# Block-sparse attention feeding a gated FFN on one core: attention scheduled in half batches, with smaller gathers issued earlier and a copied second key tile

## The chip, the cores and the metric

One core of one Trainium2 chip. Times are device microseconds (us) of that core, of whole executions; a profile is of one such execution. The engines are called here as in the profile: PE (TensorE matmuls), PEld (its weight loads), DVE (VectorE), ACT (ScalarE), POOL (GpSimd) and SP (SyncE, which here only issues DMAs).

## The reference, cut to what matters

Four batches, eight heads, 768 positions, head size 64. A query block of 32 positions sees its neighbours, the first and the last block, and three sampled blocks; the first and the last query block see everything. The attention output, 3072 tokens of 512, goes through a gated FFN.
```python
def _attn_ref(q, k, v, sampled_blocks):          # (4, 8, 768, 64) each
    scores = np.matmul(q, k.transpose(0, 1, 3, 2)) / np.sqrt(D)
    mask = np.abs(blk_i - blk_j) <= 1            # blocks of 32
    mask = mask | (blk_i == 0) | (blk_j == 0) | (blk_i == n_blocks - 1) | (blk_j == n_blocks - 1)
    for qb in range(n_blocks):
        for kb in sampled_blocks[qb]:            # three per query block
            mask[qb * block:(qb + 1) * block, kb * block:(kb + 1) * block] = True
    # ... softmax over the masked scores
    return np.matmul(attn, v)

def _moe_ref(x, w_gate, w_val, w_out):           # x (3072, 512), w (512, 1536), (1536, 512)
    gate = 1.0 / (1.0 + np.exp(-(x @ w_gate)))
    return gate * (x @ w_val) @ w_out
```

## The kernel before

Four head pairs of four batches are 16 units of attention. For each unit PE transposes K and Q (`turn`), POOL gathers the sampled key blocks and the "second key tile" of each query tile (the two blocks that follow its first key tile, the first and the last block) into `kg`, and likewise for the values into `vg`. Five score steps (`x` = 0 to 4) each go through an exponential on ACT, the first three also through a mask multiply on DVE. `values` multiplies with V for three of the six query tiles, `x_turn` transposes the result for the FFN. The order in which the program emits the instructions of one engine matters: in the traces below they run in it.

```python
    def gather_k(u):
        t = work.tile([128, NKI, BLK], f16, tag="kg", bufs=2, name="kg")
        data = kT[u].bitcast(u32).rearrange("p (n r) -> p n r", r=BLK // 2)
        for i in range(2):
            nc.gpsimd.indirect_copy(
                # ... 45 of the 90 blocks: 720 words a partition, from data by idx[:, i, 0:3]
            )

    def gather_v(u):
        # ... two indirect_copy, one a head: 30 blocks, 960 words a partition

    def scores(u, x):
        # ...
        if x < 3:
            for i in range(2):
                # ...
                mm(i, 0, kT[u][:, t * 128 : t * 128 + 128], qs, n)
                c = (3 * NQ + 4 * t) * BLK
                mm(i, n, kg[u][:, c : c + 128], qs, n)      # the second key tile, gathered

    def pieces(b):                                          # attention of one whole batch
        # ...
        def prep(u):
            return [
                lambda: (turn(u, "k"), gather_k(u)),
                lambda: (turn(u, "q"), gather_v(u)),
            ]
        r += prep(first)
        for u in us:
            # ... score steps of u, values of u - 1, prep(u + 1) if u is not the last

    spread_v(0, 0)
    spread_v(0, 1)
    head = pieces(0)
    for i, s in enumerate(head):                            # all of batch 0 first
        s()
        if i in (3, 6, 9):
            load_w(i // 3 - 1)
    # ... loads of batch 1 and of the output weights

    for b in range(B):                                      # FFN of batch b beside attention of b + 1
        g = 2 * b
        if b == 0:
            items = [s for two in zip(ins(0), ins(1)) for s in two] + outs(0)
        else:
            items = mix(ins(g), lag) + mix(ins(g + 1), outs(g))
        lag = outs(g + 1)
        # ...
        steps = pieces(b + 1) if b + 1 < B else []
        lo, hi = (0.5, 0.97) if b == 0 else (0.05, 0.95)
        # ... the steps are strewn among the items between the shares lo and hi
```

The softmax here doesn't subtract the row's maximum and nothing guards it: scores larger than these inputs give would overflow.

## Time and profile before

| | before |
|---|---|
| median of the three runs before the prediction, and the two fast ones | 419.06 us; 415.95 and 419.06 (the third took 766.75 us) |
| profiled execution | 416.7 us, mean granted clock 0.913 |
| first FFN matmul | 85.6 us |
| PE waiting for the gathered keys | 57.1 us |

The last line is the total of the view of waits. The first view is from part 2 of the page: PE's busy tenths in 40 slices of 10.4 us, and the granted clock of PE.

```profile
PE   1140656899744876969189999959699999999984
...
PEclk9999756589968999998869999979699999999999
```

PE is nearly full only from the 22nd slice on, with dips at the 27th and the 29th. The clock line dips where PE had been idle. It says nothing of the first slices: the clock record in the trace begins at 44.2 us, and the view counts what stands before as full speed. The windows view cuts the same execution at the first FFN matmul and at the end of the last attention; its columns are the stretch, its length, busy time of each engine with its count of instructions, the granted clock, the DMA share and GB/s.

```profile
0.00:85.60 85.60, 38.76 (x633) 29.53 (x634) 34.56 (x84) 23.94 (x25) 44.48 (x48) 0.82 0.80 114
85.60:351.40 265.80, 216.71 (x2647) 134.04 (x2646) 121.50 (x230) 101.06 (x143) 101.95 (x86) 0.92 0.48 82
351.40:416.70 65.30, 58.01 (x309) 29.93 (x307) 20.78 (x35) 12.28 (x25) 0.00 (x0) 1.00 0.12 41
```

The middle has PE busy 216.7 of 265.8 us at a clock of 0.92. Who PE waited for from the first FFN matmul on (total us, times, longest):

```profile
PE st L296 <- POOL kg L262: 34.8, 8, 9.9
```

One such wait, in order of time (start, us, what it was, and in brackets the idle time before it and what ended it):

```profile
295.54 0.39 PE L296 MATMUL st<-qz,kg 128*128 128x256 f16 x1 [4.67 <-POOL kg L262]
...
296.15 1.48 PE L434 MATMUL gv<-x,wg 128*128 128x384 f16 x4
297.43 1.48 PE L434 MATMUL gv<-x,wv 128*128 128x384 f16 x4
```

After 4.67 us of idle PE is slow: four matmuls of 384 columns take 1.28 us from start to start (296.15 to 297.43) where an undisturbed group takes 0.65. The spacing is back to normal after 300 us, so this wait cost some 7 us: 4.67 us idle and about 2.3 us of slow work (an estimate: half of the 4.7 us until then). A key gather is short (1.20 us for 720 words), but 2.1 to 2.4 us stand before each in which POOL does nothing else, mostly put down to "issue". POOL needs 14.3 us a unit in the stretch where it is busiest:

```profile
129.05 1.21 POOL L262 INDIRECT_COPY kg<-kT,idx 128x720 uint32 x1 [2.35 <-issue]
...
143.36 1.21 POOL L262 INDIRECT_COPY kg<-kT,idx 128x720 uint32 x1 [2.07 <-DVE xs L410]
...
157.98 1.44 POOL L262 INDIRECT_COPY kg<-kT,idx 128x720 uint32 x1 [2.08 <-DVE xs L410]
```

These are the first key gathers of the last three units of batch 1; the three other gathers of each unit stand between them. They follow each other with no room for PE to run ahead, and the attention of a batch is only about 22 us of PE work: this stretch runs at POOL's pace.

### The profile page before, as it was taken

What the parts mean: (1) busy time and instruction counts of PE and PEld (TensorE: products, weight loads), DVE (VectorE), ACT (ScalarE), POOL (GpSimd) and SP (SyncE); (2) the same over time, 40 slices, a digit from 0 to 9 for tenths busy, and PEclk for the clock granted to TensorE, in tenths of its full rate; (3) what the DMA queues carried; (4) which work ended last, traced back from release to release, by engine and by line L of the source; (5) the groups of instructions that cost most, each with busy time, mean ns of one, the idle gap of its engine ahead of it and who ended that gap; (6) DMA issues with size and microseconds to landing.
All of it is one profiled execution on the core that took longest, in us unless ns stands there. A gap on an engine that the chain in (4) does not pass through costs nothing.

```text
span 416.7 us, 8409 instructions
## 1 busy us (share of the span) xinstructions
PE 313.5 (75%) x3584; PEld 193.5 (46%) x3584; DVE 176.8 (42%) x349; ACT 137.3 (33%) x193; POOL 146.4 (35%) x133
## 2 busy tenths in 40 slices
PE   1140656899744876969189999959699999999984
PEld 1030534655422654635056666525366665555541
DVE  6230534433422564444135655435266554333321
ACT  1040343423324444225125454125154551222200
POOL 8415533680043544850443359024433410000000
PEclk9999756589968999998869999979699999999999
DMA  9979750299940000898500109666101000101102
GB/s 123 208 156 172 114 95 2 36 158 212 199 91 2 2 2 2 118 208 178 140 0 28 27 27 146 144 154 140 37 27 27 27 4 26 50 25 28 50 28 76
DMA packets 67046, 34.23 MB, mean 82 GB/s; under 512 B 28352, under 2 KB 63936, under 8 KB 67008
## 3 DMA queue, kind: packets, MB, share of 16 engines
q0 software_dynamic: 36368, 14.16, 28.8%
q1 hardware_dynamic: 30640, 19.53, 19.4%
q8 instruction: 28, 0.46, 0.5%
q14 instruction: 10, 0.08, 0.1%
HBM read 28.57 MB, written 6.29 MB: 84 GB/s over the span
## 4 chain that ended last, share of the span: by engine, by line
PE 53%; issue 12%; POOL 11%; DMA 9%; DVE 8%; ACT 3%; SPq 2%; DVEq 0%; POOLq 0%
PE gv L434 23%; PE py L454 14%; PE st L296 7%; DMA v<-va 7%; POOL kg L262 6%; PE pv L357 6%; POOL vg L277 3%; SPq L144 2%; ACT pt L331 2%; PE ptr L245 2%; DVE pt L342 2%; DVE kT L251 1%; DMA va<-in_v_dram 1%; POOL va L135 1%; DVE y L463 1%
## 5 line engine op out<-in xcount | busy, mean ns | idle before, releaser
L331 ACT ACTIVATE pt<-st 128x1024 f16<-128x1024 f32 (+1 forms) x80 | 79.8, 1002 | 148.3 <-PE st L296 148.2
L296 PE MATMUL st<-qz,kg 128*128 128x64 f16 (+1 forms) x448 | 45.5, 228 | 62.9 <-POOL kg L262 57.1
L342 DVE TENSOR_TENSOR pt<-pt,mask 128x1024 f16<-128x1024 f16 (+1 forms) x64 | 39.4, 636 | 115.5 <-ACT pt L331 115.4
L277 POOL INDIRECT_COPY vg<-v,idx 128x960 uint32 x32 | 57.8, 1807 | 76.6 <-issue 48.1
L445 DVE SCALAR_TENSOR_TENSOR h<-tg,gv 128x384 f16<-128x384 f32 x96 | 53.1, 553 | 74.0 <-PE gv L434 66.3
L434 PE MATMUL gv<-x,wg 128*128 128x384 f16 x384 | 82.4, 339 | 0.0
L434 PE MATMUL gv<-x,wv 128*128 128x384 f16 x384 | 80.7, 334 | 1.8 <-DVE h L445 1.0
L443 ACT ACTIVATE tg<-gv 128x384 f32<-128x384 f32 x96 | 47.0, 490 | 100.1 <-PE gv L434 86.7
L262 POOL INDIRECT_COPY kg<-kT,idx 128x720 uint32 x32 | 39.4, 1232 | 109.8 <-issue 51.4
L454 PE MATMUL py<-wo,h 128*128 128x512 f16 x288 | 75.5, 389 | 2.9 <-DVE y L463 2.9
L296 PEld LDWEIGHTS <-kg 128*128 128x128 f16 x448 | 26.5, 106 | 79.8 <-POOL kg L262 64.3
L434 PEld LDWEIGHTS <-wv 128*128 128x128 f16 x384 | 38.4, 100 | 32.7 <-issue 10.4
L434 PEld LDWEIGHTS <-wg 128*128 128x128 f16 x384 | 36.8, 101 | 25.3 <-issue 3.8
L296 PE MATMUL st<-qz,kT 128*128 128x256 f16 (+1 forms) x192 | 39.0, 277 | 11.9 <-DVE qz L256 9.6
L454 PEld LDWEIGHTS <-h 128*128 128x128 f16 x288 | 26.3, 100 | 27.7 <-issue 5.7
L357 PEld LDWEIGHTS <-pt 128*32 128x32 f16 (+2 forms) x1280 | 32.3, 107 | 8.9 <-DVE xs L410 3.5
L357 PE MATMUL pv<-vg,pt 128*32 128x65 f16 (+2 forms) x896 | 31.7, 207 | 0.0
L357 PE MATMUL pv<-va,pt 128*64 128x65 f16 (+1 forms) x384 | 25.7, 207 | 2.7 <-DVE xs L410 2.7
L296 PEld LDWEIGHTS <-kT 128*128 128x128 f16 x192 | 17.9, 110 | 12.9 <-DVE kT L251 5.5
L135 POOL DMA_DIRECT2D va<-in_v_dram x24 | 21.2, 911 | 0.0
L463 DVE TENSOR_SCALAR y<-py 128x512 f32<-128x512 f32 x24 | 16.5, 688 | 11.0 <-PE py L454 10.9
L410 DVE TENSOR_TENSOR xs<-pv,rz 128x384 f16<-128x384 f32 x32 | 17.8, 557 | 1.1
(44 smaller groups left out, 154.1 us busy)
## 6 DMA issues: line engine op xcount, KB each, us to landing
v<-va SPq DMA_DIRECT2D x128, 99.0 KB, 2.4
out_dram<-y SPq DMA_DIRECT2D x20, 256.0 KB, 2.0
k<-in_k_dram POOLq DMA_DIRECT2D x16, 192.0 KB, 6.2
q<-in_q_dram POOLq DMA_DIRECT2D x16, 192.0 KB, 6.8
va<-in_v_dram POOLq DMA_DIRECT2D x24, 128.0 KB, 5.4
wg<-in_moe_w_gate_dram POOLq DMA_DIRECT2D x3, 512.0 KB, 5.7
wv<-in_moe_w_val_dram POOLq DMA_DIRECT2D x3, 512.0 KB, 7.5
wo<-in_moe_w_out_dram POOLq DMA_DIRECT2D x3, 512.0 KB, 12.2
```

Source lines behind the costliest of these rows:

```text
L135: nc.gpsimd.dma_start(va[b % 2][:, m, :, 0:D], v[b, :, m * 128 : m * 128 + 128].rearrange("h p d -> p h d"),)
L262: nc.gpsimd.indirect_copy(t.rearrange("p n r -> p (n r)") .bitcast(u32) .rearrange("p (n r) -> p n r", r=BLK // 2)[:, 45 * i : 45 * i + 45 ...
L277: nc.gpsimd.indirect_copy(vg[u % 2][hd] .rearrange("p n e -> p (n e)") .bitcast(u32) .rearrange("p (n e) -> p n e", e=VE // 2)[:, :, 0 : D ...
L296: nc.tensor.matmul(st[:, bank, col : col + n], keys, qs, start=True, stop=True)
L331: nc.scalar.activation(pt[:, 0:w], st.rearrange("p a n -> p (a n)")[:, 0:w], AF.Exp, scale=SCALE)
L342: nc.vector.tensor_tensor(pp, pp, mk.unsqueeze(2).to_broadcast([128, 2 * nt, 2, nq]), op=ALU.mult)
L357: nc.tensor.matmul(pvv[rows, tl, hd, :], pr, val[:, 0:65], start=first[0], stop=False, skip_group_check=True, **({} if pos is None else {" ...
L434: nc.tensor.matmul(t, w[:, i, f * 128 : (f + 1) * 128], xT[g, i], start=(i == 0), stop=(i == NP - 1),)
L443: nc.scalar.activation(tg, pgs.pop((g, f)), AF.Tanh, scale=0.5)
L445: nc.vector.scalar_tensor_tensor(h_, tg, 1.0, pvv_.pop((g, f)), op0=ALU.add, op1=ALU.mult)
L454: nc.tensor.matmul(pys[g, tt], hts[g, f][:, tt * 128 : (tt + 1) * 128], wo[:, f], start=(f == 0), stop=(f == NF - 1),)
L463: nc.vector.tensor_scalar_mul(y, pys.pop((g, tt)), 0.5)
```

## The change

Its intent: put only half of batch 0's attention before the FFN, run attention half a batch ahead of the FFN from then on, and take gathers off PE's path. A unit is now a half batch and a head pair (32 units of three query tiles). The second key tile is copied by DVE (`kb`) and the second value tile by DMA (`second_v`), so the gathers hold sampled blocks only, one gather for keys and one for values of both heads; they are emitted two units ahead, and K is transposed three units ahead.

```diff
-    def spread_v(b, half):
+    def spread_v(b, hh, eng):
         for a in range(4):
-            for s in range(4):
+            for s in range(3):
...
+    def second_v(b, half):
+        n = 3 if half == 0 else 2
+        t = work.tile([128, 3, H, VE], f16, tag="vb", bufs=2, name="vb")
...
+    load_qk(0, 0, "k")
+    load_qk(0, 0, "q")
+    for i in range(NZ):
+        nc.vector.memset(qz[i], 0.0)
+        if i < 2:
+            nc.vector.memset(va[i][:, :, :, D:VE], 1.0)
+            nc.gpsimd.memset(v4[i], 0.0)
...
-            t = work.tile([128, S], f16, tag="kT", bufs=3, name="kT")
+            t = work.tile([128, S], f16, tag="kT", bufs=5, name="kT")
...
+            s = work.tile([128, NT - 1, 128], f16, tag="kb", bufs=5, name="kb")
+            tb = t.rearrange("p (n r) -> p n r", r=BLK)
+            nc.vector.tensor_copy(
+                s[:, :, 0:64], t.rearrange("p (m c) -> p m c", c=128)[:, 1:NM, 0:64]
+            )
...
-        t = work.tile([128, NKI, BLK], f16, tag="kg", bufs=2, name="kg")
+        n = 3 * (RS[half][1] - RS[half][0]) + 2
+        t = work.tile([128, 38 * BLK], f16, tag="kg", bufs=4, name="kg")
...
-                mm(i, n, kg[u][:, c : c + 128], qs, n)
+                mm(col + n, kb[b, p][:, min(i, NT - 2)], qs, n)
...
+    def ahead(w):
+        r = []
+        b, i = divmod(w, 2 * NP)
+        for b2, p in ((b + 1, i - 5), (b, i + 3)):
+            if 0 <= p < NP and 0 < b2 < B:
+                r.append(lambda b2=b2, p=p: turn(b2, p, "k"))
...
+        if w + 2 < NW and w + 2 >= NP:
+            r.append(lambda: (gather_k(w + 2), gather_v(w + 2)))
...
+    spread_v(0, 1, nc.scalar)
+    second_v(0, 0)
+    load_w(1)
...
+    for g in range(2 * B):
+        items = mix(ins(g), outs(g - 1) if g else [])
...
+        todo = steps(g + 1) if g + 1 < 2 * B else []
+        lo, hi = 0.04, 0.92
```

## The prediction

> **What bounds the kernel now.** TensorE, but only part of the time. In the windows view 220 to 267.6 us has TensorE busy 45.8 of 47.6 us at clock 1.00. The head is not so: 0 to 80 us has it busy 35 us, with the clock at 0.59 to 0.69 after 40 us, and the first FFN matmul starts at 85.6 us, because all of batch 0's attention comes first, paced by gathers and loads. 112 to 220 us is broken too. PE waits for the kg gather: 27.6 us before 120 us, 20.5 us from 120 to 220, then 4.3 and 4.7 us in the batch at 267 to 353. The Trainium skill (TensorE: Matmul & The Clock Gate, Part 1) says an idle window of about 3.4 us halves the clock. The trace agrees: after the 4.7 us wait that ends at 295.5 us, 8 FFN matmuls take 2.56 us instead of 1.30.
>
> **Dense work.** From undisturbed spacings: FFN input 1.30 us per 8 matmuls, x96 = 125; output 0.87 us per 4, x72 = 62; attention about 11 us per half batch. Sum 276 us; so 140 of 417 us are not dense work.
>
> **What changes.**
> - Only half of batch 0's attention precedes the FFN; then half g+1 runs beside FFN g. Matmul count unchanged.
> - A unit's first score step needs no gather (the second key tile is a VectorE copy), and gathers are issued two units ahead: the waits at batch starts, and the slow clock after them, should vanish.
> - Gathers: still 64, but 608/512 words instead of 720, 768/640 instead of 960. At 1.67 ns a word (1.20 us per 720) plus 2.1 us of issue each: 3.05 and 3.3 us, 51 us a batch (before 54). With 10.5 us of load issues POOL needs 31 us a half against PE's 35 to 37: close, but hidden.
> - Added: 32 VectorE key copies (estimate 0.4 us each), 32 small ones; 30 copy DMAs a batch instead of 32.
> - Against it: two 6660-element memsets on POOL ahead of most loads. VectorE took 0.70 us for 768; at that rate 6 us each, so v loads 12 us later.
>
> **The sum.**
> - Head, limited by POOL's queue: loads and memsets to 25 us, 8 gathers and 6 weight issues to 58; first FFN matmul at 62 us (before 85.6).
> - FFN half 0: dense 27 us, but POOL owes gathers for units 4 to 7 and 13 us of load issues: 36 us.
> - Halves 1 to 6: 35.3 us dense at the 0.965 of the good stretch: 36.6 x 6 = 220.
> - Half 7, tail, last store: 39.
> - Total 357 us.
>
> Fast runs of before are 416 to 419. I predict 357 us, 338 to 382 in 8 of 10. Chances: faster by over 2% 0.97, within 2% 0.02, slower 0.01.
>
> **What would show each step.** First FFN matmul near 62 us. PE's wait for kg under 15 us after the head; clock 0.97 or more from 110 us on. FFN halves spaced 35 to 38 us. POOL gathers spaced 3.0 to 3.4 us; memsets 5 to 8 us each. After the last attention about 31 us of pure FFN (before 60).
>
> **What would make it wrong.** POOL memsets much slower. K loads of the next batch reaching the transposes late (issued one and a half units ahead): PE stalls and cools each batch, 8 us a time. POOL falling behind when VectorE operations with two SBUF inputs hold it: the Trainium skill (SBUF — State Buffer, Who interferes with whom) says they share a port; a 0.69 us mask multiply took 2.77 us at 43 us, which agrees. Then halves are POOL-paced at 40 us and the total is 380. A head ready by 52 us would give 345.

## The result

| | before | changed |
|---|---|---|
| median | 418.13 us of four runs, 417.21 us of the three fast ones | 359.29 us |
| range | 415.95 to 419.06 (fast runs) | 357.03 to 360.37 |
| ratio, 95% interval | | 0.8601 (0.8532 to 0.8669) |
| profiled execution | 416.7 us | 358.2 us |
| first FFN matmul | 85.6 us | 72.0 us |

A ratio is the mean time of one kernel's runs over that of the other's of the same rounds, so not quite the ratio of the medians. Executions over 1.5% slower than the fastest of the same kernel are left out of the means. The same views after, first part 2 of the page (slices of 9.0 us):

```profile
PE   1026006598989999999999999899999999999983
...
PEclk9999999999999999999999999999999999999998
```

PE is at 8 or 9 from the ninth slice to the 38th. The windows view, cut again at the first FFN matmul and, as half 7 begins, at the end of the last attention:

```profile
0.00:72.00 72.00, 21.77 (x356) 17.29 (x357) 41.98 (x80) 13.71 (x17) 43.70 (x41) 1.00 0.86 129
72.00:318.10 246.10, 238.75 (x3063) 154.22 (x3062) 161.09 (x317) 119.65 (x180) 100.13 (x95) 1.00 0.54 92
318.10:358.20 40.10, 32.42 (x169) 16.25 (x167) 11.49 (x19) 5.88 (x12) 0.00 (x0) 0.97 0.14 47
```

Now the middle has PE busy 238.8 of 246.1 us. Waits of PE from the first FFN matmul on:

```profile
PE py L487 <- DVE y L496: 2.3, 3, 0.8
PE st L357 <- POOL kg L308: 1.4, 1, 1.4
```

The wait for gathered keys went from 34.8 us (same stretch before) to 1.4 us. Two gathers of one unit and the first of the next, on POOL:

```profile
99.53 1.10 POOL L308 INDIRECT_COPY kg<-kT,idx 128x608 uint32 x1 [2.30 <-DMA vb<-va]
101.96 1.43 POOL L322 INDIRECT_COPY vg<-v,idx 128x768 uint32 x1 [1.32 <-issue]
105.15 1.10 POOL L308 INDIRECT_COPY kg<-kT,idx 128x608 uint32 x1 [1.76 <-issue]
```

A unit of three query tiles takes POOL 5.6 us when gathers follow each other, so 11.2 us for the six tiles that took 14.3 us before. The first FFN matmuls of the changed kernel:

```profile
72.00 1.49 PE L467 MATMUL gv<-x,wg 128*128 128x384 f16 x4
73.28 1.49 PE L467 MATMUL gv<-x,wv 128*128 128x384 f16 x4
```

They too run at half speed (1.28 us for four), although the windows view gives a clock of 1.00 for the 72 us before and for the stretch they lie in. That 1.00 is no measurement: the clock record of this trace begins at 76.2 us, with full speed. Before it the spacing must do, and it says half speed through the whole head: score matmuls of 256 columns start 0.21 us apart from 18 to 75 us and 0.11 us apart at 88 us. By spacing, groups of four FFN input matmuls that took over 0.95 us number 11 in the records of before, the last at 297 us, and 3 in those of the changed kernel, the last at 75 us. All 14 lie in a recorded half-speed stretch or before the record begins.

Where did 58 us come from? Take the dense PE work from undisturbed spacings as the prediction did: 276 us in all, of which 22 us (before) or 11 us (changed), estimates from the same spacings, stand ahead of the first FFN matmul.

| | before | changed |
|---|---|---|
| until the first FFN matmul | 85.6 us, of them not dense work 63.6 | 72.0 us, not dense work 61.0 |
| from there to the end | 331.1 us for 254 us of work, 77 lost | 286.2 us for 265 us of work, 21 lost |

The head became shorter by about as much as its work, and loses nearly as much as ever. Counted as lost time, 2.6 us of the gain is in the head and 56 us behind it.

In the changed head, two things stand out that the prediction had not seen. The first is a conversion of 66 numbers on DVE, the first line here from DVE's timeline of the kernel before:

```profile
4.50 0.20 DVE L174 CAST sf<-sbi 128x66 f32<-128x66 uint16 x1 [1.53 <-DMA sbi<-in_sampled_blocks_dram]
```

The same in the changed kernel:

```profile
5.03 8.99 DVE L194 CAST sf<-sbi 128x66 f32<-128x66 uint16 x1
```

And the memsets that POOL ran beside it, with the load that stood behind them:

```profile
2.71 11.26 POOL L182 MEMSET v<- 128x6660 f16 x2
13.88 0.64 POOL L122 DMA_DIRECT2D k<-in_k_dram  x1
```

It took 8.99 us instead of 0.20, and ended at 14.02 us, just after the two memsets did at 13.97. What this alone cost is not separated: e1 below moves the memsets, and with them both the conversion and the loads. The second is ACT, held by the copies that it issues for the second half of V:

```profile
37.27 14.59 ACTq L141 DMA_DIRECT2D v<-va  x11
51.96 0.79 ACT L297 COPY qz<-ptr 64x768 f16<-64x768 f16 x1 [16.91 <-DMA v<-va]
```

The next score step of PE in the same timeline:

```profile
53.80 0.37 PE L357 MATMUL st<-qz,kT 128*128 128x256 f16 x1 [17.48 <-DVE qz L298]
```

The ACT half of the Q copy of unit 2 stands in ACT's order behind 11 DMA issues that took 14.59 us, DVE's half follows it, and PE waits 17.48 us for it. Meanwhile POOL, done with its key gathers and weight issues at 40.8 us, waits for the copies of V before its first value gather:

```profile
50.71 1.44 POOL L322 INDIRECT_COPY vg<-v,idx 128x768 uint32 x1 [9.94 <-DMA vb<-va]
```

### The profile page after: what moved, and what is told of

The parts are those of the page before. It is cut to its first block, busy times and chain, and to the rows that moved or that the text cites. A ratio compares the mean times of both kernels' runs of the same rounds, so it can differ in the third digit from the quotient of the medians.

```text
span 358.2 us, 8505 instructions
## 1 busy us (share of the span) xinstructions
PE 292.9 (82%) x3584; PEld 187.8 (52%) x3584; DVE 214.6 (60%) x416; ACT 139.2 (39%) x209; POOL 143.8 (40%) x135
## 4 chain that ended last, share of the span: by engine, by line
PE 68%; DVE 9%; DMA 7%; POOL 6%; ACT 4%; issue 3%; SPq 1%; ACTq 0%; POOLq 0%
PE gv L467 32%; PE py L487 16%; PE st L357 9%; PE pv L410 6%; DMA v<-va 5%; ACT pt L382 4%; POOL v L182 3%; PE ptr L276 3%; DMA va<-in_v_dram 2%; DVE pt L392 2%; PE ptx L455 2%; DVE qz L298 2%; DVE y L496 1%; POOL va L130 1%; DVE xs L445 1%
## 5 line engine op out<-in xcount | busy, mean ns | idle before, releaser
L382 ACT ACTIVATE pt<-st 128x1024 f16<-128x1024 f32 (+2 forms) x96 | 82.2, 863 | 91.2 <-PE st L357 91.2
L392 DVE TENSOR_TENSOR pt<-pt,mask 128x1024 f16<-128x1024 f16 x64 | 44.2, 690 | 47.4 <-ACT pt L382 47.1
L308 POOL INDIRECT_COPY kg<-kT,idx 128x608 uint32 (+1 forms) x32 | 37.4, 1169 | 85.1 <-DVE h L478 22.6
L322 POOL INDIRECT_COPY vg<-v,idx 128x768 uint32 (+1 forms) x32 | 46.8, 1461 | 51.6 <-issue 33.9
L357 PE MATMUL st<-qz,kT 128*128 128x128 f16 (+1 forms) x192 | 36.1, 251 | 24.8 <-DVE qz L298 18.9
L410 PEld LDWEIGHTS <-pt 96*32 96x32 f16 (+2 forms) x1280 | 30.6, 102 | 6.6 <-ACT pt L382 1.0
L298 DVE COPY qz<-ptr 64x768 f16<-64x768 f16 x16 | 15.4, 961 | 23.0 <-ACT qz L297 22.8
L357 PE MATMUL st<-qz,kb 128*128 128x256 f16 (+1 forms) x96 | 25.9, 285 | 0.0
L357 PE MATMUL st<-qz,kg 128*128 128x64 f16 x352 | 21.9, 200 | 4.7 <-POOL kg L308 3.4
L357 PEld LDWEIGHTS <-kb 128*128 128x128 f16 x96 | 9.9, 103 | 29.9 <-issue 25.2
L297 ACT COPY qz<-ptr 64x768 f16<-64x768 f16 x16 | 12.7, 792 | 31.0 <-DMA v<-va 16.9
L357 PEld LDWEIGHTS <-kg 128*128 128x128 f16 x352 | 18.9, 103 | 10.0 <-POOL kg L308 4.0
```

Of the source, the lines that this page charges most:

```text
L298: nc.vector.tensor_copy(z[D:128, :, 1], tok[D:128])
L308: nc.gpsimd.indirect_copy(words(t, BLK // 2)[:, 0:n], words(kT[b, p], BLK // 2), idx[:, half, 0 : 3 - half], i_know_this_is_slow=True,)
L322: nc.gpsimd.indirect_copy(words(t, VE // 2)[:, 0 : 2 * n, 0 : D // 2], words(v4[p // 2][:, p % 2 * 2 * VE : p % 2 * 2 * VE + 6528], D // 2 ...
L357: nc.tensor.matmul(st[:, col : col + n], keys, qs, start=True, stop=True)
L382: nc.scalar.activation(pt[:, 0:n], st[:, 0:n], AF.Exp, scale=SCALE)
L392: nc.vector.tensor_tensor(pp, pp, mk.unsqueeze(2).to_broadcast([128, nt, 2, nq]), op=ALU.mult)
```

## The experiments

All kernels gave correct results. The medians stand beside the changed kernel's 359.29 us; ratios to the kernel before of the same rounds are given where two kernels come close. With an interval of about 0.005 on a ratio, and the median of the kernel before between 415.97 and 419.16 us in the rounds of the experiments, differences under some 3 us are not settled. Line numbers differ a little between kernels; L350 and L357 are both the score matmuls.

Theory 1: the gain comes from PE waits on gathers that disappear, through the lead of the gathers and through a first score step that needs none. Rival 2: it comes from the half-batch lag, by the earlier FFN start and by slack. Theory 3, about the head: it is paced by POOL's queue (memsets, loads), against the copies and ACT.

### Lag undone (e5_whole_batch)

```diff
-        t = work.tile([128, GT], f16, tag=f"x{p}", bufs=2, name=f"x{p}")
+        t = work.tile([128, GT], f16, tag=f"x{p}", bufs=4, name=f"x{p}")
...
+    for s in steps(1):
+        s()
     for g in range(2 * B):
...
-        todo = steps(g + 1) if g + 1 < 2 * B else []
+        todo = steps(g + 2) if g + 2 < 2 * B else []
...
-        if g % 2 == 1 and g // 2 + 2 < B:
+        if g % 2 == 0 and g // 2 + 2 < B:
             load_batch(g // 2 + 2)
```

> Only the half-batch lag is undone: the attention of both halves of batch 0 stands before the first FFN matmul and attention runs two halves ahead of the FFN; gathers, copies and their lead stay as changed. Worked out from the changed kernel's trace: first FFN matmul at 97 to 102 us (gathers 4 to 7 and 13 us of load issues on POOL come first), then 28 us, five halves of 35.5, 24 and 40: total 366 to 372. Rival (the lag gave most of the 58 us): total 390 or more.

Measured: 378.34 us, 19 us more; first FFN matmul at 101.7 us, as expected, and the total above the range expected (the profiled execution, 375.22 us with a span of 373.4, was the shortest of the six). From 101.7 to 334 us PE is busy 225.5 of 232.3 us, so the middle stays full without the lag. The lag is worth about a third of the gain; the rival's 390 or more is out.

### No lead at batch starts (e4_late_first)

```diff
+        if i == 0 and b > 0:
+            r.append(lambda: (turn(b, 0, "k"), gather_k(w), gather_v(w), gather_k(w + 1), gather_v(w + 1)))
         for b2, p in ((b + 1, i - 5), (b, i + 3)):
-            if 0 <= p < NP and 0 < b2 < B:
+            if 0 <= p < NP and 0 < b2 < B and (p > 0 or i < 5):
...
-        if w + 2 < NW and w + 2 >= NP:
+        if w + 2 < NW and w + 2 >= NP and (w + 2) % 8 > 1:
```

> The changed kernel, but the key transpose of each batch's first unit (batches 1 to 3) comes at the start of that unit instead of three units before, with its gathers and those of the second unit right behind: no lead at batch starts, as in the kernel before. Theory L (the lead of the gathers removed the batch-start waits and the slow clock behind them): PE waits for kg 3 to 6 us three times, clock below 0.97 near 106, 178 and 250 us, total 369 to 383. Rival H (the half-batch lag alone did it): no wait over 1.5 us, total within 3 us of 359.

Measured: 366.32 us, 7 us more, between what the two theories expected. The waits did not come back as they were:

```profile
PE gv L467 <- DVE h L478: 4.1, 4, 1.3
PE st L357 <- POOL kg L308: 2.7, 4, 1.5
```

The wait for keys is 2.7 us in all, and no FFN group after 75 us is at half speed. So this experiment alone does not confirm theory 1: without the lead the first score step, which needs no gather, and the FFN items after it cover most of the gather. By the starts of the FFN halves, most of it lies in halves 3 and 5, beside which batches 2 and 3 begin: 36.8 us each instead of 33.95, of which 1.3 us is one wait for DVE's products and about 1 us is PE work moved there from other halves (half 4 is 1.2 us shorter). The rest is spread over small waits.

### Second key tile gathered again (e6_key_gather)

```diff
+    for t in range(NT - 1):
+        c = 36 + 4 * t if t < 3 else 94 + 4 * (t - 3)
+        lk[:, c : c + 4] = [4 * t + 4, 4 * t + 5, 0, NB - 1]
...
-            s = work.tile([128, NT - 1, 128], f16, tag="kb", bufs=5, name="kb")
...
-        n = 3 * (RS[half][1] - RS[half][0]) + 2
+        n = 48 if half == 0 else 38
...
-                mm(col + n, kb[b, p][:, min(i, NT - 2)], qs, n)
+                c = (36 + 4 * i if half == 0 else 30 + 4 * (min(i, NT - 2) - 3)) * BLK
+                mm(col + n, kg[w][:, c : c + 128], qs, n)
```

> Only the copied second key tile is undone: its four blocks per query tile are gathered again (800/640 words instead of 608/512), and the first score step waits for the gather as before. The lead of the gathers stays. Theory S (with the lead the gather is there in time): waits of PE on kg under 4 us after the head, total 359 to 363. Rival K (the copy is what removed the waits): total 370 or more.

Measured: 362.34 us (ratio 0.8665 against 0.8601). PE waits 3.0 us for keys after the first FFN matmul, once, in half 0. That is theory S: with the lead, the copy is worth at most some 3 us, which is at the edge of what these rounds resolve.

### Both: gathered tile and no lead (e7_key_gather_late)

The edits of e4 and e6 together.

> e6 and e4 together: gathered second key tile and no lead at batch starts, which is how the kernel before starts a batch, but within the half-batch schedule. If copy and lead each cover for the other, this costs more than the sum of both alone (e4 was 7 us): PE waits 4 to 6 us for kg three times with the slow clock after each, total 374 to 386. If they are independent: 7 us plus what e6 costs.

Measured: 382.42 us, 23 us more, against 7 + 3 for the two alone. Waits of PE for keys from the first FFN matmul on:

```profile
PE st L350 <- POOL kg L301: 15.4, 6, 4.8
```

One of them in order of time, with the FFN group after it:

```profile
117.52 0.39 PE L350 MATMUL st<-qz,kg 128*128 128x256 f16 x1 [3.21 <-POOL kg L301]
...
121.60 1.47 PE L461 MATMUL gv<-x,wg 128*128 128x384 f16 x4
```

The first line is the total, 15.4 us. In the second pair PE idles 3.21 us for the gathered keys at a batch start, and the FFN group after it takes 1.47 us instead of 0.81: the wait and the slow clock of the kernel before are back. Each of the three batch starts has this wait of 3.21 us; a slow FFN group follows two of them (121.6 and 275.7 us), none the one that ends at 196.1 us. Lead and copy each cover for the other; removing both shows what they are worth together, about 23 us. The expectation of three waits of 4 to 6 us was too high: after 145 us there are four waits, of 7.4 us together, so part of the 23 us is shorter waits and slow matmuls that are not listed one by one.

### All three undone (e9_three_undone)

The edits of e5 and e7 together.

> Half-batch lag, copied key tile and lead at batch starts undone together (e5 + e7). If the lag is independent of the other two, the costs add: 19 us (e5) + 23 us (e7) on 359 = 401, range 397 to 405, and 13 to 21 us of the whole gain are left for the rest of the change (value gather without the second tile, larger pools). If the whole-batch schedule gives the late gathers more to hide behind, less: 385 to 395.

Measured: 397.36 us, 38 us more (19 + 23 = 42 by addition), at the low end of the additive range. So lag, lead and copied key tile account for 38 of 58 us. About 20 us remain between this kernel and the one before (417.00 us in these rounds). They lie in what was not undone: single gathers for both heads without the second value tile, four gather buffers instead of two, K transposed further ahead, the different order of the head. The first FFN matmul of e9 is at 102.6 us, later than the 85.6 us of before, and it still is 20 us faster, so they lie behind the head: there e9 is 37 us shorter (294.2 against 331.1 us), and its head gives 17 us back. Waits of PE for keys from the first FFN matmul on:

```profile
PE st L350 <- POOL kg L301: 9.6, 3, 3.2
```

Before they were 34.8 us, so 25 of these 37 us are waits for gathers again. The shorter POOL time of a unit (11.2 against 14.3 us for six tiles) fits, but no run here separates these parts.

| undone | median, us | more than 359.29 |
|---|---|---|
| copied key tile (e6) | 362.34 | 3 |
| lead at batch starts (e4) | 366.32 | 7 |
| both (e7) | 382.42 | 23 |
| half-batch lag (e5) | 378.34 | 19 |
| all three (e9) | 397.36 | 38 |

### How much slack POOL has (e11_double_gather)

```diff
-        nc.gpsimd.indirect_copy(
+        for _ in range(2 if w >= 12 else 1):
+            nc.gpsimd.indirect_copy(
...
```

> The changed kernel with every key gather from unit 12 on done twice (same result): 4 x 2.6 = 10.4 us more POOL work in each of the last five halves that gather, so 38 us against a TensorE half of 34 to 37. If POOL is hidden with 8 us to spare as the spacing of its gathers says, this costs 3 to 15 us in all (362 to 374). If POOL was already the pace of the halves, 45 us or more. If the slack is larger than it looks, under 2 us.

Measured: 364.30 us, 5 us for 20 extra gathers that were 2.6 to 3.7 us apart from their twins, over 50 us of POOL work: nearly all of it fits into slack. What it cost shows where slack ends, in PE's timeline:

```profile
221.90 0.85 PE L276 MATMUL ptr<-ident,k 96*64 96x96 f16 x16 [4.51 <-DMA k<-in_k_dram]
...
225.22 1.49 PE L468 MATMUL gv<-x,wg 128*128 128x384 f16 x4
```

The gathers delay the load of the next batch's first K, which stands behind them in POOL's order, and PE waits 4.51 us once for the transpose and then runs an FFN group at half speed. This is the failure that the prediction had feared for the change itself.

### The head: memsets to DVE (e1_memset_dve)

```diff
-            nc.gpsimd.memset(v4[i], 0.0)
+            nc.vector.memset(v4[i], 0.0)
```

> The two memsets of the value tiles move from POOL (5.67 us each, loads behind them start at 13.9 us) to VectorE (estimate 3.0 us each from 0.70 us per 768 words). Theory A, the head is paced by POOL's queue: every load comes 11 us earlier, the sf cast no longer takes 9 us, first FFN matmul at 61 to 64 us instead of 72.0, total 348 to 351. Theory B, the head is paced by the copy DMAs and the blocked ACT queue: the loads come earlier but FFN starts at 69 us or later, total 355 to 359.

Measured: 352.99 us (ratio 0.8508, about 4 us better by the ratios, though their intervals overlap), between the two theories; first FFN matmul at 61.5 us, which is what theory A said. The conversion on DVE took 0.23 us again, and each memset there 2.83 us. But the 10.5 us gained at the first FFN matmul did not all last: FFN half 0 (from the first FFN matmul of half 0 to that of half 1) took 39.3 us instead of 33.6, with one wait of PE for keys of 5.85 us, and the gain at the start of half 1 was 4.8 us.

### The head: copies from SP (e2_spread_sp)

```diff
-    spread_v(0, 1, nc.scalar)
     second_v(0, 0)
+    spread_v(0, 1, nc.sync)
```

> The second spread of batch 0 is issued from SP behind the second_v copies instead of from ACT, whose queue was held from 37 to 52 us while PE waited 17.5 us for the q copy behind it. Theory B (the ACT block costs): that wait of PE falls under 4 us, scores of units 2 and 3 are done before their gathers, first FFN matmul at 64 to 67 us, total 351 to 354. Theory C (the copies themselves are the limit, whoever issues them): PE waits for the value gathers instead, FFN starts at 70 to 75 us, total 357 to 362.

Measured: 357.44 us, ratio 0.8588 against 0.8601: the same. First FFN matmul at 64.5 us, as theory B said. The waits of PE, whole execution:

```profile
PE pv L410 <- DMA vb<-va: 9.0, 1, 9.0
PE st L357 <- POOL kg L308: 8.2, 2, 6.1
```

The wait of 17.5 us is now 2.2 us, as expected, and others are there: 9.0 us for the `second_v` copies and 6.1 us once for keys in half 0. Half 0 took 39.8 us, and half 1 began at 104.3 us instead of 105.6. Theory B's total, 351 to 354 us, is missed; the total is theory C's, and PE does wait for copies of V instead. So ACT's block was real and cost the first FFN matmul 7.5 us, but hardly the total.

### Both (e3_both)

The edits of e1 and e2 together.

> Both edits. If the two costs are separate they add: first FFN matmul at 54 to 58 us, total 340 to 346. If they are the same wait seen twice, no better than the better one of the two alone, within 2 us.

Measured: 351.45 us (ratio 0.8451, about 6 us better). First FFN matmul at 58.0 us, at the late edge of what was expected for separate costs; half 0 took 41.0 us. The expectation named the total of 340 to 346, and it is missed: 351.45 us is within 2 us of e1 alone, as the other side, one wait seen twice, had it. The costs add at the first FFN matmul and not in the total: in half 0 POOL issues the loads of batch 1 and of the output weights in one block between gathers that PE needs. From its POOL timeline:

```profile
52.08 1.43 POOL L322 INDIRECT_COPY vg<-v,idx 128x768 uint32 x1 [10.69 <-issue]
...
59.83 1.32 POOL L322 INDIRECT_COPY vg<-v,idx 128x640 uint32 x1 [1.11 <-issue]
...
75.58 1.02 POOL L308 INDIRECT_COPY kg<-kT,idx 128x512 uint32 x1 [1.48 <-issue]
```

POOL also sat 10.69 us before 52.08 us, waiting for the second spread, whose last copy landed at 50.4 us. The next key gather after 59.83 us is at 75.58 us, and PE waited 7.8 us for it.

### Loads of batch 1 earlier (e8_early_loads)

e3 with the loads of batch 1 put into that gap, and the output weights behind the gathers of unit 5.

```diff
     load_w(2)
+    load_qk(1, 0, "k")
+    load_qk(1, 0, "q")
+    load_v(1)
...
-    load_batch(1)
+    load_qk(1, 2, "q")
+    load_qk(1, 3, "q")
+    gather_k(5)
+    gather_v(5)
     for s in range(3):
         load_wo(s)
-    gather_k(5)
-    gather_v(5)
```

> e3 (351.5 us) with the loads of batch 1 issued while POOL waits for the second spread (41 to 52 us there) and the output weights behind the gathers of unit 5. Theory: FFN half 0, 40 us in e3 because POOL owes 13 us of load issues plus gathers, falls to 28 to 32 us; first FFN matmul stays at 58 to 61 us; total 341 to 346. Rival: the loads slow the spread's DMAs and FFN starts after 64 us: total 348 or more.

Measured: 348.55 us (ratio 0.8324). The total is the rival's. Both sides were half right on the way: half 0 fell to 32.2 us, and the first FFN matmul slipped to 63.3 us, with PE waiting 10.0 us for a value gather that stood behind the loads.

### POOL's order in the head (e10_head_order)

e3 with the key gathers of units 4 and 5 in the gap instead, weights later, and the loads of batch 1 in pieces. The lines that take the same calls out of their old places are cut.

```diff
     gather_v(0)
     gather_v(1)
+    gather_k(4)
+    gather_k(5)
+    load_w(1)
...
     gather_v(3)
...
+    load_qk(1, 0, "k")
+    load_qk(1, 0, "q")
     gather_v(4)
...
+    load_w(2)
+    load_v(1)
+    gather_v(5)
+    for p in range(1, NP):
+        load_qk(1, p, "k")
+        load_qk(1, p, "q")
+    for s in range(3):
+        load_wo(s)
```

> e3 (351.5 us) with POOL's order in the head changed: key gathers of units 4 and 5 go into the 10.7 us in which POOL waits for the second spread, the second and third weight slices come after, the loads of batch 1 come after the last value gather of the head and in pieces between gathers. Theory: first FFN matmul at 53 to 58 us (the spread no longer shares the DMA engines with weight loads), half 0 at 30 to 34 us instead of 40, total 340 to 345. Rival, as in e8: what leaves the head comes back as a wait for batch 1's loads or for the weights in half 0: total 347 or more.

Measured: 346.62 us (344.43 to 348.27, ratio 0.8314, 95% interval 0.8264 to 0.8365). It beats the kernel before by 17% and the changed one by 3%; against e8 it is not separated. First FFN matmul at 52.8 us, half 0 at 40.6 us. It was expected at 30 to 34 us. Waits of PE from 55 to 100 us:

```profile
PE ptr L276 <- DMA k<-in_k_dram: 3.8, 1, 3.8
PE ptr L276 <- DVE x L457: 2.7, 1, 2.7
```

The windows view settles where half 0 went: PE is busy 31.9 of its 40.6 us and waits 8.7, against 30.6 and 3.0 us in the changed kernel, for the same 438 matmuls. So 7 of the 19 us that left the head came back, most of it in the two waits shown, the larger one for a K load of batch 1 as the rival said. What the six kernels have in common is the time from the start of half 1 to the end:

| | first FFN matmul | start of half 1 | from there to the end |
|---|---|---|---|
| changed | 72.0 | 105.6 | 252.6 |
| e1 | 61.5 | 100.8 | 249.7 |
| e2 | 64.5 | 104.3 | 252.3 |
| e3 | 58.0 | 99.0 | 249.4 |
| e8 | 63.3 | 95.4 | 253.1 |
| e10 | 52.8 | 93.4 | 253.0 |

(profiled executions, us.) The first FFN matmul moved by 19 us and the start of half 1 by 12. Half 1 begins when its own attention, which runs beside FFN half 0, is done, and that waits for what POOL issues in order: in half 0 PE waits once for keys in e1, e2 and e3 (5.85, 6.1 and 7.8 us) and once for a K load in e10 (3.8 us). The first FFN matmul is a milestone on the way, not the limit.

## Why the prediction was right

The total was predicted as 357 us and came out at 359.29, but its terms were off in both directions, and that they cancelled is luck.

| term | predicted | profiled |
|---|---|---|
| head, to the first FFN matmul | 62 us | 72.0 us |
| FFN half 0 | 36 us | 33.6 us |
| FFN halves 1 to 6 | 220 us (36.6 each) | 212.5 us (35.4 each) |
| half 7, tail, last store | 39 us | 40.1 us |
| sum | 357 us | 358.2 us |

- **Mechanism of the middle: right.** PE's wait for keys after the head is 1.4 us (under 15 was said). The clock record is at 1.00 from 76.2 us to the end of the matmuls, and spacing confirms it there: no slow FFN input group after 76 us. Halves took 33.8 to 38.1 us, the lower ones below the 35 to 38 predicted, because the loss factor of 0.965 taken from the good stretch before was too careful. By e5, e7 and e9 these savings are shared: the lag 19 us, lead and copied tile together 23 us, some 20 us not separated. The prediction had not said how much each part is worth.
- **POOL hidden: right, with more room than said.** A unit's two gathers take 5.6 us, not the 6.4 predicted, because I charged each gather with the 2.1 us of issue seen before; between gathers of one unit the profile shows 1.1 to 1.3 us. e11 put in over 50 us of POOL work for 5 us.
- **Head: the term that was mis-sized, by 10 us.** The step that failed is "Head, limited by POOL's queue". POOL's memsets were sized well (5.67 us each, 6 predicted). The loads were issued by 23.9 us, as predicted (25). But behind them the head does not follow POOL's count of instructions: the copies of V were not in the sum, and the first value gather waited 9.9 us for them, while ACT was held 14.6 us by issuing half of them. e2, with these issues off ACT, moves the first FFN matmul by 7.5 us. e1 moves it by 10.5 us, but that is the memsets' time, which the sum had counted.
- **Half 0: right in kind.** The prediction said that POOL owes gathers and load issues there, and e1, e2, e3 and e10 show that it takes back 6 to 7 us of what is gained in the head (half 0 at 39.3 to 41.0 us instead of 33.6); e8, which moves loads out of half 0, does not (32.2 us).
- **Last attention to the end: small miss.** From the last FFN half to the end of its matmuls is 35 us, 31 predicted; the last output groups wait three times 0.8 us for DVE in both kernels.

The Trainium skill was drawn on in two places of the prediction. TensorE: Matmul & The Clock Gate, Part 1, says that an idle window of about 3.4 us halves the clock: agreed, e.g. 4.67 us idle and then 1.28 us for four matmuls instead of 0.65, and 4.51 us idle in e11; of the three waits of 3.21 us in e7 two were followed by it. SBUF — State Buffer, Who interferes with whom, says that DVE's copies and casts in its two-port modes and POOL lock each other out for a whole instruction. I used the section's rule for operations with two SBUF inputs, for mask multiplies in the middle, where it did not matter (POOL stayed hidden, and in the example it was DVE that was held, not POOL), and not this one for the memsets at the start, where the cast took 8.99 us instead of 0.20. e1 shows that it was the memsets: without them the same cast took 0.23 us.

Two more pages explain experiments after the fact. VectorE: DVE Perf Modes, Zero memsets can be issued as uint32, says that a Vector-engine memset takes one cycle per element and can be issued on 4-byte words: in e1 the same zeroes appear as 3330 words in 2.83 us on DVE, against 6660 half words in 5.67 us on POOL, 0.85 ns an element in both. The number of cycles is not measured here. DMA: Bandwidth & Descriptors, Issuing engines are not separate DMA queues, says that spreading DMAs over issuing engines does not add bandwidth: moving 12 of the 24 copies of batch 0's two spreads from ACT to SP left the landing of the last one where it was, 54.6 us in the changed kernel and 53.7 us in e2, which agrees.

What stays open: which part of the change gives the last 20 us between e9 and the kernel before; and how the 7 us of e4 divide between its small waits and moved work.

## What to carry to other kernels

When PE is the goal, ask for each of its waits what else could fill it: a lead of the gathers and a first step that needs no gather were worth 7 and 3 us alone but 23 us together, so undoing one part of a change understates it. An earlier milestone is not an earlier end; check the next point at which the slow engine's whole debt is due. Put nothing long on a queue whose later instructions are on the path: not memsets ahead of loads, and not a dozen DMA issues ahead of a copy that PE needs.

## What the Trainium skill lacked or had wrong

- No page that I read gives the cost of POOL's indirect copy. Here 512, 608 and 720 words a partition took 1.02, 1.10 and 1.20 us for keys, 640 and 768 words 1.32 and 1.43 us for values, which is not in proportion to the words. Where gathers of the changed kernel follow each other, 1.1 to 1.8 us stand before each in which POOL does nothing else.
- GPSIMD Engine Reference, Common operations, names memset without a rate, and no page says whether the reference's general figures per element hold for it. Here 6660 two-byte elements took 5.67 us, 0.85 ns each.
- SBUF — State Buffer, Who interferes with whom, says that the loser is blocked for the whole instruction, but not what happens when another follows at once. Here the DVE cast was held over two memsets in a row: begun at 5.03 us, in the first of them, it ended at 14.02 us, after the second. The second was recorded as begun 0.08 us before the first ended.
- TensorE: Matmul & The Clock Gate, Part 1, warns that recorded clock events are not always reliable, but not that a record is silent before its first event. Here it begins at 44.2 us (before) and 76.2 us (changed), and matmuls ahead of that run at half speed by their spacing; from there on, record and spacing agree for every FFN input group of both kernels.

